# S4D convolution and gated GLU on one core: regrouped spectra transfers and a back transform in two rounded parts

## The chip, the cores and the metric

The kernel runs on one core of a Trainium2 chip. The metric is device time in microseconds (us) of one execution. A core has TensorE (PE, matrix products into the accumulator banks of PSUM), VectorE (DVE), ScalarE (ACT), GpSimd (POOL) and SyncE (SP, which here only issues transfers), and 16 DMA engines that move data between the on-chip memory (SBUF, 128 partitions) and DRAM. SP, ACT and POOL each have a queue of instructions of their own and can issue transfers from it.

## The reference, cut to what matters

```python
xn = layernorm(A_u)                                  # (1, 2048, 448)
dt = exp(log_dt); A = -exp(log_A_real) + 1j*A_imag   # A, C: (448, 256)
C  = (C_real + 1j*C_imag) * dt[:, None]
P  = exp((A*dt[:, None])[:, :, None] * arange(2048)) # (448, 256, 2048)
K  = 2 * einsum("dn,dnl->dl", C, P).real             # kernel of the convolution
y  = irfft(rfft(xn^T, 4096) * rfft(K, 4096), 4096)[:, :, :2048]^T + xn*D_skip
B  = (sigmoid(xn @ w_gate) * (xn @ w_up)) @ w_down   # 448 -> 1792 -> 448
return A_u + y + B                                   # all float32
```

## The kernel before, in words

Two generators are interleaved by weights that they yield: `conv` (the S4D part) and `glu` (the gated GLU). Their instructions go to the same engines. Within an engine's queue the order is fixed when the program is built; `issue_after` ties the matmuls of one generator behind those of the other.

**GLU.** It runs in two halves of the tokens. `gate` (line 661) makes the gate and up products: 11 matmuls of 512 columns for each of the two, since operands are split into a rounded part and a remainder (`wh`, `wl`, `xh`, `xl`, type F32R, which TensorE takes in one pass). ACT and DVE make `th`, `hf`, `hh`, `hl`. The down products `po` (line 781) are of 448 columns in the same split, and DVE adds them to `acc` (line 786).

**Convolution, first part** (`kgen`, to about 580 us). The kernel K is generated and put through the first stage of its transform, in 14 banks of 32 channels. After each bank `first_stage` writes the tile `sk` to the DRAM tensor `sk_d` (line 540, ACT queue, 512 KB each).

**Convolution, second part** (`spectra`, line 803). 16 steps: two halves h of the channels (224 each), and in each eight values of k (0, 4, ..., 28), four frequencies k1 to a step. One step is:

- `loads` (line 822), issued three steps ahead on SP: `sx`, the spectrum of the input, in two transfers (lines 826, 827); `tb`, a table (829); `skl`, the spectrum of the kernel (831). In `sk_d` a partition's part of `skl` lies in seven runs of 512 bytes.
- `there` (line 840): matmuls `sp` (line 854) into PSUM for two values of j, ACT copies one of them to `kc` (862), DVE multiplies the two complex spectra into `yy` (lines 865 to 868). The results of the two j lie in two tiles.
- `back` (line 872) for the step before: matmuls `pv` of `yy` with the table `bk` (line 880), both plain float32, 224 columns. Each of the 8 calls appears in the trace as two instructions. Partitions 0 to 63 and 64 to 127 are two independent products. ACT copies the results to `vt` (886), and four SP transfers write `vt` to `v_d` in DRAM (892).
- `turned` (line 894): one SP transfer of 448 KB brings the step's share of `v_d` back as `vp`, 16 partitions of 28,672 bytes, one step later. Its DRAM side is `v_d[h, k//4::8]`, 16 rows of 28,672 bytes each.

When all eight `vp` of a half are there, `last` (line 900) makes the final matmuls (909), DVE adds them to `ac` or `acc` (917), and `out` (line 214) writes finished tokens, taking SP, ACT and POOL in turn. For h = 0 the four calls of `last` come in the two steps after the last `turned` of that half is issued (`due = [n + 1]`, line 954). For h = 1 they come at the very end (line 799), behind the last GLU matmuls. GLU matmuls stand between `there` of a step and `back` of the next.

Of the kernel before, what the change touches and what calls it, by code (L numbers as in the profile page):

```python
# [20 lines left out]
D = 448  # L21
N = 256
F = 1792
NA = 32
NB = 64
NK1 = 32
# [13 lines left out]
H = D // 2  # L40
RB = 2
# [14 lines left out]
def _tables():  # L56

    a = np.arange(NA)[:, None]
    b = np.arange(NB)[:, None]
    k1 = np.arange(NK1)[None, :]  # L60
    ang = 2 * np.pi * ((a * (4 * k1 + 1)) % 128) / 128.0

    wk = np.zeros((4, NA, 2, 2, NK1))
    wx = np.zeros((4, NA, 2, NK1))
    for j in range(4):
        wk[j, :, 0, j % 2] = wx[j, :, 0] = np.cos(ang)
        wk[j, :, 1, j % 2] = wx[j, :, 1] = -np.sin(ang)
# [10 lines left out]
    split = lambda t: t.reshape(64, 2, 32).transpose(0, 2, 1)  # L78
    both = lambda r, i: np.stack([split(r), split(i)], 3).reshape(64, 128)
# [21 lines left out]
    f = lambda v, s: np.ascontiguousarray(v.reshape(s).astype(np.float32))  # L101
    return {
        "c_wk": f(wk, (128, 2, 64)),
        "c_wx": f(wx, (128, 64)),
        "c_tab": f(tab, (8, 128, 4, 128)),
        "c_bk": f(bk, (128, 2, 128)),
        "c_wf": f(wf, (128, 32, NA)),
        "c_sel": f(sel, (128, 2, 512)),
        "c_id": np.eye(128, dtype=np.float32),
    }  # L110
# [3 lines left out]
def s4d_glu_kernel(ctx, tc, io):  # L114
    nc = tc.nc
    hp = tc.high_priority
    v = nc.vector
# [93 lines left out]
    def blocks(t, g, b0, nb):  # L211
        return t[g, :, b0 // 8, b0 // 4 % 2, b0 % 4 : b0 % 4 + nb]

    def out(src, b0, h):

        ds = slice(H * h, H * h + H)
        for g in range(4):
            eng = (nc.sync, nc.scalar, nc.gpsimd)[outs[0] % 3]
# [206 lines left out]
    def kgen(pk):  # L425
# [95 lines left out]
        def first_stage(bank):  # L521

            ks, sk = tl["ks"], tl["sk"].rearrange("p k (s r j) -> p r k s j", r=2, j=2)

            pss = [
                psc[-1].tile([128, 8, 2, 32], F32, name="kp", bufs=1),
                psg.tile([128, 8, 2, 32], F32, name="kq", tag="gu", bufs=4),
            ]
            for s_ in range(8):
                for cc in range(2):  # L530
                    for r in range(2):
                        rows = slice(64 * r, 64 * r + 64)
# [7 lines left out]
            nc.scalar.dma_start(sk_d[:, bank], tl["sk"])  # L540

        with hp(HP):
            phase_load(0)
# [259 lines left out]
    def spectra(pf):  # L803
# [1 line left out]


        wf = const.tile([128, 32, NA], F32, name="wf", tag="sel", bufs=1)
        bk = const.tile([128, 2, 128], F32, name="bk", tag="wk", bufs=1)

        vp = {0: pf.tile([128, 32, H], F32, name="vp", bufs=1)}  # L810
        spare = {
            "vt": [pf.tile([128, 2, 2, H], F32, name="vt", bufs=2)],
            "pd": [pf.tile([128, 2, H], F32, name="pd", bufs=2)],
            "yy": [pf.tile([128, 2, H], F32, name="yy", bufs=4)],
            "kc": [pf.tile([128, 2, H], F32, name="kc", bufs=3)],
        }

        def work(n, sh, bufs):
            return spare[n].pop() if spare[n] else pf.tile(sh, F32, name=n, bufs=bufs)


        def loads(h, k):
            sx = pf.tile([128, 4, H], F32, name="sx", bufs=NLD)
            sk = pf.tile([128, 7, 4, 32], F32, name="skl", bufs=NLD)
            ds, gs = slice(H * h, H * h + H), slice(7 * h, 7 * h + 7)
# [5 lines left out]
            nc.sync.dma_start(sk, sk_d[:, gs, k : k + 4])  # L831
            return tb, sk, sx

        def bank(name):
            return psc[-1].tile([128, 2, H], F32, name=name, tag="sp", bufs=4)

        def after():
            return tc.issue_after(sp_mm[0].ins)

        def there(tb, sk, sx):  # L840

            ys_ = []
            for j in range(2):
                pss = []
                for src in (sk, sx):
# [14 lines left out]
                    if src is sk:  # L860
                        kc = work("kc", [128, 2, H], 3)
                        nc.scalar.copy(kc, ps)
                yy, pd = work("yy", [128, 2, H], 4), work("pd", [128, 2, H], 2)
                xt = pss[1]
                v.tensor_tensor(yy, kc, xt, ALU.mult)
                v.tensor_tensor(pd, kc, xt[:, ::-1], ALU.mult)
                v.tensor_tensor(yy[:, 0], yy[:, 0], yy[:, 1], ALU.subtract)
                v.tensor_tensor(yy[:, 1], pd[:, 0], pd[:, 1], ALU.add)
                ys_.append(yy)
            return ys_  # L870

        def back(h, k, ys_):
            vt = work("vt", [128, 2, 2, H], 2)
            pvs = [bank("pv") for _ in range(2)]
            with after():
                for j in range(2):
                    for e in range(2):
                        for i in range(2):
                            s = slice(64 * i, 64 * i + 64)
                            mm = nc.tensor.matmul(  # L880
                                pvs[i][:, j], bk[s, e], ys_[j][s, e], start=(e == 0), stop=(e == 1),
                                skip_group_check=True,
                            )
            sp_mm[:] = [mm]
            for i in range(2):
                nc.scalar.copy(vt[:, i], pvs[i])

            for j in range(2):
                for i in range(2):
                    k1 = k + 2 * j + i  # L890
                    to = v_d[h, 8 * (k1 % 4) + k1 // 4 :: 32]
                    nc.sync.dma_start(to.rearrange("r w d -> w r d"), vt[:, i, j])

        def turned(h, k):
            if h not in vp:
                vp[h] = pf.tile([128, 32, H], F32, name="vp", bufs=1)
            s = slice(k // 4, 128, 8)
            nc.sync.dma_start(vp[h][s], v_d[h, s])

        def last(h, m):  # L900

# [29 lines left out]
        for n, (h, k) in enumerate(steps):  # L931
# [167 lines left out]
```

## Time and profile before

| | |
|---|---|
| median of 3 runs | 773.14 us (771.35 to 775.21) |
| the profiled execution | 770.64 us |
| its span, first to last instruction | 768.9 us |
| mean granted TensorE clock | 0.968 |
| busy: PE, PEld, DVE, ACT, POOL | 705.4, 555.6, 557.4, 420.3, 359.7 us |
| bytes moved by DMA | 114.31 MB in 89575 packets |

The page of the profile gives each engine's busy time over the span, a strip of 40 equal slices, the DMA queues, the chain of work that ended last, and the costliest groups of instructions (line, engine, operation, output <- inputs, count | busy us, mean ns | idle time ahead of them and its releaser). PEld is the loading of weights into TensorE. A view by windows gives busy times in stretches of the span, the granted clock, the DMA share (mean busy share of the 16 DMA engines; packets of one engine may overlap, so it can pass 1) and GB/s. An "SPq" or "ACTq" row is an instruction of that queue, such as the issue of a transfer; where the chain says "DMA", the time runs from issue to landing.

### The profile page before, as it was taken

The page shows a single profiled execution, that of the slowest core. Times are in us where ns is not written, and L with a number is a line of the kernel's source. Part 1 is how long each engine was busy: PE and PEld are TensorE (multiplying, and loading weights), DVE is VectorE, ACT ScalarE, POOL GpSimd, SP SyncE. Part 2 cuts the span into 40 slices and gives each one's busy share as a digit, 9 for nine tenths or more (in the row PEclk, how much of TensorE's full clock was granted, in tenths as well). Part 3 has the DMA queues.
Part 4 walks back from the last instruction along what each step waited for, and adds up shares of the span by engine and source line. Part 5 has one row for each costly group of instructions (what it writes and reads, how often), then busy time and mean ns, then how long its engine had stood idle before and what let it go on. Part 6 is the DMA issues. An engine that isn't in the chain of part 4 may idle for free.

```text
span 768.9 us, 19294 instructions
## 1 busy us (share of the span) xinstructions
PE 705.4 (92%) x7868; PEld 555.6 (72%) x7868; DVE 557.4 (72%) x768; ACT 420.3 (55%) x647; POOL 359.7 (47%) x423
## 2 busy tenths in 40 slices
PE   2798899997999999898999999999899999969994
PEld 1575688876877877565788887887777778746783
DVE  5779996798978998778478977877864554634553
ACT  3636364767677976777387667686552322312320
POOL 1101036896785788853437584486555002331001
PEclk9998899999999999899999999999999999989998
DMA  9936337334323542363962232222157999999846
GB/s 205 227 81 187 95 93 230 101 122 151 120 70 126 185 135 67 108 189 92 269 182 69 68 124 66 90 94 67 41 142 199 283 240 238 230 241 242 189 127 161
DMA packets 89575, 114.31 MB, mean 149 GB/s; under 512 B 10896, under 2 KB 77456, under 8 KB 89232
## 3 DMA queue, kind: packets, MB, share of 16 engines
q1 hardware_dynamic: 80176, 92.36, 45.3%
q10 hardware_dynamic: 6736, 14.57, 6.3%
q0 software_dynamic: 2576, 6.17, 3.1%
q8 instruction: 62, 1.02, 0.6%
q14 instruction: 25, 0.20, 0.1%
HBM read 69.21 MB, written 43.84 MB: 147 GB/s over the span
## 4 chain that ended last, share of the span: by engine, by line
PE 40%; DMA 16%; DVE 15%; ACT 10%; POOL 9%; issue 7%; SPq 2%; ACTq 1%; POOLq 0%; DVEq 0%
PE gu L674 13%; PE po L781 11%; PE tr L506 4%; PE sp L854 4%; PE ko L582 3%; POOL me L483 3%; PE pv L880 2%; DVE pm L420 2%; DMA sx<-x_d 2%; DVE Et L569 2%; DVE Et L568 2%; ACT S L518 2%; POOL mf L483 2%; DVE Ft L570 2%; ACT S L516 1%
## 5 line engine op out<-in xcount | busy, mean ns | idle before, releaser
L483 POOL TENSOR_TENSOR me<-me,pm 128x32 f32<-128x32 f32 (+1 forms) x168 | 135.5, 807 | 99.5 <-DVE Et L569 88.1
L483 POOL TENSOR_TENSOR mf<-mf,pm 128x64 f32<-128x64 f32 (+1 forms) x112 | 118.0, 1054 | 4.5
L674 PE MATMUL gu<-xh,wh 128*128 128x512 f32 x336 | 101.3, 408 | 5.2 <-ACT xh L201 5.2
L569 DVE TENSOR_TENSOR Et<-me,S 128x1024 f32<-128x1024 f32 x56 | 80.0, 1429 | 24.5 <-ACT me L496 20.0
L674 PE MATMUL gu<-xh,wl 128*128 128x512 f32 x336 | 96.9, 394 | 0.0
L674 PE MATMUL gu<-xl,wh 128*128 128x512 f32 x336 | 96.6, 391 | 0.0
L781 PE MATMUL po<-dh,hh 128*128 128x448 f32 x224 | 87.3, 390 | 4.4 <-DVE acc L786 2.5
L568 DVE TENSOR_TENSOR Et<-me,S 128x1024 f32<-128x1024 f32 x56 | 77.9, 1391 | 16.8 <-ACT S L518 16.6
L690 ACT CAST hh<-hf 128x512 fp32r<-128x512 f32 x56 | 34.9, 623 | 98.9 <-DVE hf L685 74.7
L570 DVE TENSOR_TENSOR Ft<-mf,S 128x1024 f32<-128x1024 f32 x56 | 80.2, 1433 | 9.6 <-ACT S L518 7.4
L781 PE MATMUL po<-dl,hh 128*128 128x448 f32 x224 | 84.7, 379 | 0.0
L781 PE MATMUL po<-dh,hl 128*128 128x448 f32 x224 | 83.7, 376 | 0.0
L515 ACT ACTIVATE S<-tr 128x1024 f32<-128x1024 f32 x56 | 57.6, 1028 | 40.4 <-PE tr L506 34.9
L674 PEld LDWEIGHTS gu<-xh,wh 128*128 128x128 f32 x336 | 62.4, 193 | 22.1 <-ACT xh L201 6.7
L582 PEld LDWEIGHTS ko<-Et,Ft 128*32 128x32 f32 x3584 | 54.8, 112 | 28.4 <-issue 13.7
L674 PEld LDWEIGHTS gu<-xh,wl 128*128 128x128 f32 x336 | 63.2, 189 | 15.2 <-DVE pl L289 0.7
L674 PEld LDWEIGHTS gu<-xl,wh 128*128 128x128 f32 x336 | 63.2, 188 | 14.1 <-issue 0.7
L582 PE MATMUL ko<-Et,Ft 128*32 128x64 f32 x3584 | 64.9, 224 | 9.1 <-DVE Et L568 7.3
L685 DVE SCALAR_TENSOR_TENSOR hf<-th,gu 128x512 f32<-128x512 f32 x56 | 38.1, 681 | 42.3 <-PE gu L674 31.5
L506 PE MATMUL tr<-sel,ph 128*128 128x512 f32 x224 | 66.8, 419 | 1.7 <-ACT S L517 1.1
L786 DVE SCALAR_TENSOR_TENSOR acc<-po,acc 128x448 f32<-128x448 f32 x80 | 48.2, 617 | 24.4 <-PE po L781 24.3
L518 ACT ACTIVATE S<-S,hpi 128x1024 f32<-128x1024 f32 x56 | 65.5, 1169 | 0.0
(190 smaller groups left out, 1299.8 us busy)
## 6 DMA issues: line engine op xcount, KB each, us to landing
sk_d<-sk ACTq DMA_DIRECT2D x14, 512.0 KB
sx<-x_d SPq DMA_DIRECT2D x32, 224.0 KB
skl<-sk_d SPq DMA_DIRECT2D x16, 448.0 KB
v_d<-vt SPq DMA_DIRECT2D x64, 112.0 KB
vp<-v_d SPq DMA_DIRECT2D x16, 448.0 KB
wt_d<-wh SPq DMA_DIRECT2D x9, 512.0 KB
wt_d<-wl SPq DMA_DIRECT2D x9, 512.0 KB
wh<-wt_d SPq DMA_DIRECT2D x9, 512.0 KB
```

The costliest lines, as they stand in the source:

```text
L483: ins = nc.gpsimd.tensor_tensor(m[:, :, w + a : 2 * w : n], m[:, :, a:w:n], par(base + i).unsqueeze(2).to_broadcast([128, 4 * DC, w // n]) ...
L506: nc.tensor.matmul(ps[:, h], ph[:, cn % 2, 128 * h : 128 * h + 128], sel[:, i], start=(i == 0), stop=(i == 1),)
L515: nc.scalar.activation(rows(cs), pv, AF.Abs)
L518: sins[:] = [nc.scalar.activation(cs, cs, AF.Sin, scale=-TWO_PI, bias=hpi)]
L568: v.tensor_tensor(Et[:, :, :, 32:64], two(me[:, :, 32:64]), S[:, 1::-1], ALU.mult)
L569: v.tensor_tensor(Et[:, :, :, 0:32], two(me[:, :, 0:32]), S[:, 1:3, :, ::-1], ALU.mult)
L570: fts[:] = [v.tensor_tensor(Ft, two(mf), S[:, 3:5], ALU.mult)]
L582: mm = nc.tensor.matmul(ko[32 * j : 32 * j + 32, sl], Ft[:, cc, DC * h + 4 * q + j], Et[:, cc, DC * h + 4 * q + j], start=(k == 0), stop=( ...
L674: glu_mm[:] = [nc.tensor.matmul(ps, a_, b_, start=(n == 0), stop=(n == len(mm) - 1))]
L685: marks[1] = v.scalar_tensor_tensor(hf, th, 1.0, pgu[1], ALU.add, ALU.mult)
L781: glu_mm[:] = [nc.tensor.matmul(po, a_[:, bs], w_, start=(n == 0), stop=(n == 3 * fc - 1))]
L786: v.scalar_tensor_tensor(acc[:, b], po, 0.5, acc[:, b], ALU.mult, ALU.add)
```

## The change

Five things, all in or around `spectra`:

1. `sk_d`, `v_d` and the column orders of two tables (`c_wx`, `c_bk`) are laid out anew. `skl` becomes one run of 3,584 bytes per partition, while each bank's write of `sk` splits into eight runs of 512 bytes per partition. `sx` comes in one transfer instead of two. `vt` goes out in one transfer, issued from ACT, instead of four from SP. The load of `vp` stays one SP transfer into the same 16 partitions; its DRAM side is now a pattern of 4 (r) by 4 (q) runs of 28,672 bytes.
2. `back` takes the products as a rounded part `yh` and a remainder `yl`, and the table as `bk` and `bl`, all F32R: three terms (bk·yh, bl·yh, bk·yl), two tables e each, two halves of partitions, 448 columns per matmul (both j together). 12 matmuls in place of 8 calls that were 16 instructions.
3. ACT makes `yh` (a copy with rounding) and DVE makes `yl` (a subtraction), once for each j. `yh` and `yl` have one buffer each and `yy` two instead of four. `bl` is one more table to load.
4. The `out` transfers of half 0's finished `ac` go to SP alone.
5. `last` of half 0 starts one step later.

```diff
-    wx = np.zeros((4, NA, 2, NK1))
+    wx = np.zeros((4, NA, NK1, 2))
...
-    sk_d = dram.tile([128, D // 32, 32, 32], F32, name="sk_d")
+    sk_d = dram.tile([128, 2, 8, D // 64, 4, 32], F32, name="sk_d")
...
-    v_d = dram.tile([2, 128, 32, H], F32, name="v_d")
+    v_d = dram.tile([2, 8, 4, 4, 32, H], F32, name="v_d")
...
-            nc.scalar.dma_start(sk_d[:, bank], tl["sk"])
+            to = sk_d[:, bank // 7, :, bank % 7].rearrange("p e k d -> p e (k d)")
+            nc.scalar.dma_start(to, tl["sk"].rearrange("p (e k) d -> p e (k d)", k=4))
...
-            nc.sync.dma_start(sx[0:64], x1_d[k : k + 4, :, ds].rearrange("k b d -> b k d"))
-            nc.sync.dma_start(sx[64:128], x1_d[32 + k : 36 + k, :, ds].rearrange("k b d -> b k d"))
+            rows = x1_d.rearrange("(k c) b d -> (c b) k d", c=2)
+            nc.sync.dma_start(sx, rows[:, k : k + 4, ds])
...
-            nc.sync.dma_start(sk, sk_d[:, gs, k : k + 4])
+            nc.sync.dma_start(sk, sk_d[:, h, k // 4])
...
-                ys_.append(yy)
-            return ys_
+                nc.scalar.copy(yh[:, :, j], yy)
+                v.tensor_tensor(yl[:, :, j], yy, yh[:, :, j], ALU.subtract)
+            return yh, yl
...
+            terms = [(w, y, e) for w, y in ((bk, yh), (bl, yh), (bk, yl)) for e in range(2)]
             with after():
-                for j in range(2):
-                    for e in range(2):
-                        for i in range(2):
-                            s = slice(64 * i, 64 * i + 64)
-                            mm = nc.tensor.matmul(
-                                pvs[i][:, j], bk[s, e], ys_[j][s, e], start=(e == 0), stop=(e == 1),
-                                skip_group_check=True,
-                            )
+                for n, (w, y, e) in enumerate(terms):
+                    for i in range(2):
+                        s = slice(64 * i, 64 * i + 64)
+                        mm = nc.tensor.matmul(
+                            pvs[i], w[s, e], y[s, e], start=(n == 0), stop=(n + 1 == len(terms)),
+                            skip_group_check=True,
+                        )
             sp_mm[:] = [mm]
             for i in range(2):
-                nc.scalar.copy(vt[:, i], pvs[i])
-
-            for j in range(2):
-                for i in range(2):
-                    k1 = k + 2 * j + i
-                    to = v_d[h, 8 * (k1 % 4) + k1 // 4 :: 32]
-                    nc.sync.dma_start(to.rearrange("r w d -> w r d"), vt[:, i, j])
+                nc.scalar.copy(vt[:, :, i], pvs[i])
+            to = v_d[h, k // 4].rearrange("q r w d -> (r w) q d")
+            nc.scalar.dma_start(to, vt.rearrange("p j i d -> p (j i) d"))
...
-            s = slice(k // 4, 128, 8)
-            nc.sync.dma_start(vp[h][s], v_d[h, s])
+            src = v_d[h, k // 4].rearrange("q r w d -> r q (w d)")
+            nc.sync.dma_start(vp[h][k // 4 :: 8].rearrange("p w d -> p (w d)"), src)
...
-                    out(ac[:, 4 * q : 4 * q + 4], 4 * q, h)
+                    out(ac[:, 4 * q : 4 * q + 4], 4 * q, h, *([] if h else [[nc.sync]]))
...
+        nc.gpsimd.dma_start(bl, io["c_bl"])
...
-                    due = [n + 1]
+                    due = [n + 2]
```

More of the change, by code (lines that the diff above doesn't have):

```diff
@@ L63, in _tables @@
     wk = np.zeros((4, NA, 2, 2, NK1))
-    wx = np.zeros((4, NA, 2, NK1))
+    wx = np.zeros((4, NA, NK1, 2))
     for j in range(4):
-        wk[j, :, 0, j % 2] = wx[j, :, 0] = np.cos(ang)
-        wk[j, :, 1, j % 2] = wx[j, :, 1] = -np.sin(ang)
+        wk[j, :, 0, j % 2] = wx[j, :, :, 0] = np.cos(ang)
+        wk[j, :, 1, j % 2] = wx[j, :, :, 1] = -np.sin(ang)
     k2 = np.arange(64)[None, :]
@@ L77, in _tables @@
     al = 2 * np.pi * ((b * k2) % 64) / 64.0
-    split = lambda t: t.reshape(64, 2, 32).transpose(0, 2, 1)
-    both = lambda r, i: np.stack([split(r), split(i)], 3).reshape(64, 128)
+    both = lambda r, i: np.stack([r.reshape(64, 2, 32), i.reshape(64, 2, 32)], 2).reshape(64, 128)
     bk = np.zeros((2, 64, 2, 128))
@@ L101, in _tables @@
     f = lambda v, s: np.ascontiguousarray(v.reshape(s).astype(np.float32))
+    bits = bk.astype(np.float32).view(np.uint32)
+    bits = ((bits + 0x7FF + (bits >> 12 & 1)) & np.uint32(0xFFFFF000)).view(np.float32)
     return {
@@ L105, in _tables @@
         "c_tab": f(tab, (8, 128, 4, 128)),
-        "c_bk": f(bk, (128, 2, 128)),
+        "c_bk": f(bits, (128, 2, 128)),
+        "c_bl": f(bk - bits, (128, 2, 128)),
         "c_wf": f(wf, (128, 32, NA)),
@@ L212, in blocks, with out @@
         return t[g, :, b0 // 8, b0 // 4 % 2, b0 % 4 : b0 % 4 + nb]
-    def out(src, b0, h):
+    def out(src, b0, h, engs=(nc.sync, nc.scalar, nc.gpsimd)):
         ds = slice(H * h, H * h + H)
         for g in range(4):
-            eng = (nc.sync, nc.scalar, nc.gpsimd)[outs[0] % 3]
+            eng = engs[outs[0] % len(engs)]
             outs[0] += 1
@@ L807, in spectra @@
         wf = const.tile([128, 32, NA], F32, name="wf", tag="sel", bufs=1)
-        bk = const.tile([128, 2, 128], F32, name="bk", tag="wk", bufs=1)
+        bk = const.tile([128, 2, 128], F32R, name="bk", tag="wk", bufs=1)
+        bl = pg.tile([128, 2, 128], F32R, name="bl", tag="rd", bufs=RB)
         vp = {0: pf.tile([128, 32, H], F32, name="vp", bufs=1)}
@@ L813, in spectra, with work @@
             "pd": [pf.tile([128, 2, H], F32, name="pd", bufs=2)],
-            "yy": [pf.tile([128, 2, H], F32, name="yy", bufs=4)],
+            "yy": [pf.tile([128, 2, H], F32, name="yy", bufs=2)],
+            "yh": [pf.tile([128, 2, 2, H], F32R, name="yh", bufs=1)],
+            "yl": [pf.tile([128, 2, 2, H], F32R, name="yl", bufs=1)],
             "kc": [pf.tile([128, 2, H], F32, name="kc", bufs=3)],
         }
-        def work(n, sh, bufs):
-            return spare[n].pop() if spare[n] else pf.tile(sh, F32, name=n, bufs=bufs)
+        def work(n, sh, bufs, dt=F32):
+            return spare[n].pop() if spare[n] else pf.tile(sh, dt, name=n, bufs=bufs)
         def loads(h, k):
@@ L840, in there @@
         def there(tb, sk, sx):
-            ys_ = []
+            yh, yl = (work(n, [128, 2, 2, H], 1, F32R) for n in ("yh", "yl"))
             for j in range(2):
@@ L862, in there @@
                         nc.scalar.copy(kc, ps)
-                yy, pd = work("yy", [128, 2, H], 4), work("pd", [128, 2, H], 2)
+                yy, pd = work("yy", [128, 2, H], 2), work("pd", [128, 2, H], 2)
                 xt = pss[1]
```

3 lines of the change are left out of this document (2 added, 1 removed).

## The prediction, made before the changed kernel was run

> **What bounds the kernel now.** I read the page first: its list of transfers and its packet counts show what the change regroups.
>
> ```profile
> DMA packets 89575, 114.31 MB, mean 149 GB/s; under 512 B 10896, under 2 KB 77456, under 8 KB 89232
> ...
> sk_d<-sk ACTq DMA_DIRECT2D x14, 512.0 KB
> sx<-x_d SPq DMA_DIRECT2D x32, 224.0 KB
> skl<-sk_d SPq DMA_DIRECT2D x16, 448.0 KB
> v_d<-vt SPq DMA_DIRECT2D x64, 112.0 KB
> vp<-v_d SPq DMA_DIRECT2D x16, 448.0 KB
> ```
>
> 89575 - 89232 = 343 packets are of 8 KB or more, and 16 loads of vp in 16 rows of 28 KB make 256 of them: a vp load moves as 16 uncut packets. Next the view by windows, for the stretch in which the spectra run, and one ahead of it for comparison (columns: window, length, busy time and count of each engine, granted clock, DMA share, GB/s).
>
> ```profile
> 400.00:500.00 100.00, 99.53 (x1437) 82.68 (x1426) 84.07 (x93) 69.11 (x99) 61.76 (x76) 1.00 0.28 91
> 587.00:640.00 53.00, 51.62 (x381) 40.01 (x379) 29.17 (x61) 14.11 (x27) 4.24 (x4) 1.00 1.09 254
> 640.00:705.00 65.00, 56.13 (x504) 41.66 (x505) 30.70 (x62) 16.07 (x31) 21.82 (x26) 0.95 1.01 234
> 705.00:745.00 40.00, 40.00 (x291) 30.77 (x290) 21.53 (x44) 11.14 (x22) 0.00 (x0) 1.00 0.75 178
> 745.00:769.00 24.00, 13.56 (x173) 11.21 (x173) 7.46 (x13) 0.95 (x2) 4.37 (x8) 0.84 0.58 154
> ```
>
> Two things are full at once from 587 to 705 us: TensorE (51.62 of 53 us, 56.13 of 65) and the DMA engines (share 1.09 and 1.01). Earlier the DMA engines are mostly free (0.28). The chain of waits, in order of time, says which one the end hangs on.
>
> ```profile
> 641.47 8.39 DMA sx<-x_d
> ...
> 649.92 9.22 DMA skl<-sk_d
> ...
> 659.16 6.77 DMA v_d<-vt
> ...
> 666.00 8.57 DMA vp<-v_d
> ...
> 754.27 0.86 issue
> 755.13 1.09 PE pv L909 x32
> ```
>
> From 641 us on it is transfers, each needing the one before, 7 to 9 us from issue to landing; TensorE carries it again later, and the end is the last matmuls with additions and writes, 768.9 - 755.1 = 13.8 us. TensorE's own row for the one long stall, and a short step for what follows:
>
> ```profile
> 649.29 1.78 PE L880 MATMUL pv<-yy,bk 64*128 64x224 f32 x16
> 651.00 0.98 PE L854 MATMUL sp<-skl,tb 128*64 128x224 f32 x8
> ...
> 654.18 0.97 PE L674 MATMUL gu<-xh,wh 128*128 128x512 f32 x3
> ...
> 656.90 1.78 PE L880 MATMUL pv<-yy,bk 64*128 64x224 f32 x16
> ...
> 686.84 3.26 PE L909 MATMUL pv<-vp,wf 64*32 64x224 f32 x64 [7.25 <-DMA vp<-v_d]
> ```
>
> So the stage is one where TensorE just keeps up with full DMA engines, and loses 7.25 us where it must have a vp. What the change does to the DMA engines decides.
>
> **The change part by part.** *The price of a byte.* Over 587 to 745 us an engine was busy 53 x 1.09 + 65 x 1.01 + 40 x 0.75 = 153.4 us and moved (53 x 254 + 65 x 234 + 40 x 178) / 16 = 2,237 KB: 14.6 KB per busy us. In 400 to 500 us it was 91 / 0.28 / 16 = 20.3. These are my two ends.
>
> *The load of vp.* It keeps 448 KB (458,752 bytes) and 16 packets of 28.7 KB. Before, the DRAM side was 16 rows and the SBUF side 16 partitions, one packet for each DMA engine: 28.7 / 14.6 = 1.97 us. Now the DRAM side is 4 rows of 4. If a transfer is dealt to the engines by its outermost dimension, four engines carry four packets each: 4 x 1.97 = 7.87 us on those four, nothing on the other twelve. No row of this trace shows engine by engine where a transfer ran, so the ends are 1.97 us (spread as before), 4 x 28.7 / 20.3 = 5.65 us and 7.87 us. I take 7.87, since 14.6 is the rate of the very windows in which vp moves.
>
> The Trainium skill, page "DMA: Bandwidth & Descriptors", section "Why a DMA increments its semaphore by 16 and not by 1", states that rule: the number of engines is the largest one up to 16 that divides the slowest dimension of both sides, as the instruction carries it, and they are the lowest-numbered ones. By it 4 and 16 give four engines, always the same four, and the sum is the one below; without it the sum is that of the first rival. No run here shows it yet.
>
> ```profile
> L898 SPq DMA_DIRECT2D vp<-v_d x16: 511/518/1398, 609.5 to 750.2; - x16
> L540 ACTq DMA_DIRECT2D sk_d<-sk x14: 326/327/375, 191.5 to 583.0; - x14
> ```
>
> *skl and sk.* skl's seven runs of 512 bytes become one. Ends: no gain, or the step from 14.6 to 20.3 KB per us, 28.7 / 14.6 - 28.7 / 20.3 = 0.56 us per engine and load, 9.0 us for 16. I take 9.0, the upper end, since no other row has a price for a longer run; it is a tenth of what vp adds. The 14 writes of sk (191 to 583 us) lose at most as much per byte, 32.8 x (1/14.6 - 1/20.3) = 0.63 us each; a DMA share like 0.28 covers that, and nothing reads sk_d before the spectra begin.
>
> *Fewer issues.* One sx instead of two and one v_d write on ACT instead of four on SP free SP, which spends 2.60 us on the four:
>
> ```profile
> 645.89 0.51 SPq L898 DMA_DIRECT2D vp<-v_d  x1
> 646.44 2.60 SPq L892 DMA_DIRECT2D v_d<-vt  x4
> ...
> 649.92 0.38 SPq L831 DMA_DIRECT2D skl<-sk_d  x1
> ```
>
> ACT, busy 14.11 of 53 us, gains one issue per step, behind its own vt copies, so it waits for nothing else. The bytes of sx and v_d and their 896-byte runs stay. On the path I give these nothing: SP is the issuer, the engines are the limit. Were SP the limit, 2.6 us a step would be the gain.
>
> *back.* Instructions by form:
>
> ```profile
> L880 PE MATMUL pv<-yy,bk 64*128 64x224 f32 x256 | 28.5, 362 | 1.4 <-DMA bk<-in_c_bk_dram 1.4
> L865 DVE TENSOR_TENSOR yy<-kc,sp 128x448 f32<-128x448 f32 x32 | 19.8, 617 | 37.7 <-PE sp L854 36.6 <-ACT kc L862 1.1
> L862 ACT COPY kc<-sp 128x448 f32<-128x448 f32 x32 | 17.0, 533 | 14.9 <-PE sp L854 14.8
> ...
> 656.14 0.39 DVE L868 TENSOR_TENSOR yy<-pd 128x224 f32<-128x224 f32 x1
> ...
> 744.96 9.31 PE po L781 x45
> ```
>
> In the short step 16 instructions take 651.00 - 649.29 = 1.71 us, eight pairs (upper and lower 64 rows side by side) of 0.214 us. The new 448 columns in one pass are the form of po, 9.31 / 45 = 0.207 us each. Six pairs at 0.214 are 1.28 us: 0.43 us saved a step, 6.9 in 16. If the pairs did not run side by side, 12 x 0.207 = 2.48 us, 0.77 lost a step, 12.4 in all. I take the saving, since L880's own halves do run side by side.
>
> *yh and yl.* Two copies on ACT (0.53 us each by kc) and two subtractions on DVE (0.62 by yy) a step. The engines have room, but back now starts only when both j are rounded, as its first matmul spans both. In the short step DVE ends at 656.14 + 0.39 = 656.53, back starts at 656.90. Adding the first yl (0.62) and the second yh (0.53) gives 657.68, 0.8 us late, and the second yl and the handovers push it to perhaps 1.6. A step with two such groups of GLU matmuls between, 2 x 2.72 us, hides it. If about half of the 16 steps are as short as this one, it is 8 x 0.9 = 7 us; the ends are 0 and 8 x 1.6 = 13. It matters only where TensorE is the bound; where loads are late they cover it.
>
> *out and due.* This wait goes, with its 18.7 us of ACT standing still:
>
> ```profile
> ACT hh L690 <- DMA out_dram<-ac: 18.7, 1, 18.7
> ```
>
> and last of half 0 comes a step later, so the 7.25 us stall can shrink to nothing if vp is on time. The price is that SP holds back its later loads while it waits for DVE's ac; with loads three steps ahead I cost it at nothing, and at up to the 7.25 if that lead is used up. bl, 128 KB on POOL, rides beside bk.
>
> **The sum.** Four engines need, until the point that was 745 us: 153.4 - 9.0 + 15 x (7.87 - 1.97) = 232.9 busy us (15 of the 16 vp are issued by then, the last at 750.2). The share in the two full windows was (57.8 + 65.7) / 118 = 1.05, so 232.9 / 1.05 = 222 us: 587 + 222 = 809. That takes all other traffic at its old price. At the other end, with twelve engines idle half the time, everything but vp goes at 20.3 and the share is 1.09: (232.9 - 118.1) x 14.6 / 20.3 = 82.6, plus 118.1, over 1.09 = 184: 771. I take the middle, 790. Then come the last vp, 7.87 / 1.05 = 7.5, and the tail of 13.8, which the vp now releases: 811. The time outside the span is 770.64 - 768.9 = 1.7: 813 beside the profiled 770.64. The median of the runs is 2.5 above that execution, so **815 us**, with 796 and 834 from the two ends. TensorE's saving in back doesn't show in it; it waits longer for loads.
>
> **The rivals.**
>
> *First: vp still spreads over 16 engines, or its place costs nothing; faster.* Then TensorE is the bound: 7.25 and 6.9 us go, 7 come back as waits for yh and yl: 773.1 - 7 = 766, down to 759 without the waits. For it: the loads run three steps ahead, and a vp is needed only in last. Against: all these loads share SP's queue and the DMA engines were full (1.09) with vp spread, so there is no room. It decides as long as a vp load takes less than about 4 us on its busiest engine: 15 x 2 = 30 busy us more is what the 0.75 window, the 9.0 of skl and the three steps' lead can take up.
>
> *Second: four engines, but each at 20.3 KB per us.* (153.4 - 29.6 - 9.0) x 14.6 / 20.3 + 15 x 5.65 = 167.4, over 1.09 = 154: the engines are done at 741, about with TensorE. With a last vp 3.7 us longer and some waits, 768 to 785, say 776. For it: the other traffic leaves room on the shared memory. Against: the row of the last vp. It is issued at 750.2 and the matmuls that need it start at 755.13 with no wait for it left, in a window with share 0.58; even that quiet load doesn't prove a faster packet.
>
> *Third: the halves of back do not run side by side.* 12.4 + 7 - 7.25 gives 785 if vp spreads. Against: L880.
>
> **How the numbers follow.** Four engines at about the old rate 0.70 (796 to 834, some 0.05 of it above), spread vp 0.15, four fast engines 0.11, serial halves 0.04. The range 774 to 834 leaves out most of the first rival and the top, 0.2. What a measurement can tell from no change is about 0.5%, 769.3 to 777.0: faster 0.19 (first rival and a part of the second), same 0.05, slower 0.76.
>
> **What would show it.** Right: the window after 600 us has a DMA share well under 1 (twelve engines waiting) while TensorE is idle for several us in most steps, released by sx, skl or tb; a step like the short one above lasts 11 us or more instead of 7.6; the last matmuls wait for vp. back shows 12 instructions in 1.28 us, and ACT's 18.7 us wait is gone. Wrong: TensorE stays busy through 705 us and the last vp lands under 5 us after its issue; then four engines were not used, or were not short of time. If TensorE's idle time stands ahead of back with yh or yl as releaser, the operand chain was the cost.

## The result, and the profile after it

The changed kernel takes 806.35 us (median of 4 runs, 803.68 to 810.02) beside 773.79 us for the kernel before: ratio 1.043, 95% interval [1.038, 1.048]. It is slower by 33 us. The profiled execution took 803.68 us, its span is 801.9 us, the mean granted clock 0.951 (before: 0.968).

First the view by windows of the changed kernel, with the columns as in the prediction.

```profile
400.00:500.00 100.00, 98.65 (x1385) 81.67 (x1384) 83.00 (x90) 72.67 (x104) 64.37 (x77) 1.00 0.31 96
587.00:640.00 53.00, 48.31 (x349) 36.01 (x348) 29.61 (x60) 19.18 (x36) 8.43 (x10) 1.00 0.81 221
640.00:705.00 65.00, 42.12 (x266) 31.07 (x266) 32.31 (x58) 17.28 (x33) 19.07 (x22) 0.82 0.82 187
705.00:745.00 40.00, 39.72 (x364) 28.26 (x365) 25.30 (x51) 14.59 (x27) 1.73 (x2) 0.95 0.70 209
745.00:802.00 57.00, 35.89 (x319) 27.79 (x317) 22.08 (x44) 9.54 (x18) 4.42 (x8) 0.87 0.40 124
```

Between 400 and 500 us little has changed (TensorE 98.65 us of 100 beside 99.53). In 640 to 705 us TensorE is busy for 42.12 us where it was 56.13, and the DMA share has fallen from 1.01 to 0.82. Neither is full now: both wait. The clock that TensorE is granted falls as well (0.95 to 0.82), and what comes after a long gap is slower: the 12 instructions of a `back` take 2.61 us there and mostly 1.5 us elsewhere. TensorE's list of waits names the gaps, and ACT's names what is behind them.

```profile
PE pv L889 <- ACT yh L876: 27.2, 8, 8.5
...
PE pv L914 <- DMA out_dram<-acc: 9.9, 1, 9.9
```

```profile
ACT kc L869 <- DMA vp<-v_d: 12.7, 3, 6.2
...
ACT kc L869 <- DMA skl<-sk_d: 8.4, 1, 8.4
```

None of these rows stood in the lists of before. TensorE waits 27.2 us for `yh`, and ACT, which makes it, stands in front of `kc`, allegedly for a `vp`. That is odd: a copy from PSUM to `kc` doesn't read `vp`. ACT's timeline of the changed kernel, and TensorE's beside it, show what stands there.

```profile
663.72 0.97 ACT L895 COPY vt<-pv 128x448 f32<-128x448 f32 x2 [1.08 <-PE pv L889]
670.52 0.37 ACTq L897 DMA_DIRECT2D v_d<-vt  x1
670.93 0.97 ACT L869 COPY kc<-sp 128x448 f32<-128x448 f32 x2 [6.25 <-DMA vp<-v_d]
674.13 0.56 ACT L876 CAST yh<-yy 128x448 fp32r<-128x448 f32 x1 [2.23 <-DVE yy L875]
677.42 0.56 ACT L876 CAST yh<-yy 128x448 fp32r<-128x448 f32 x1 [2.73 <-DVE yy L875]
```

```profile
651.04 1.11 PE L889 MATMUL pv<-yh,bk 64*128 64x448 f32 x4 [6.29 <-ACT yh L876]
...
678.03 1.11 PE L889 MATMUL pv<-yh,bk 64*128 64x448 f32 x4 [8.46 <-ACT yh L876]
```

`vt` is ready at 663.72 + 0.97 = 664.7, but its issue to `v_d` goes out only at 670.52. ACT works in order, so `kc` and `yh` stand behind that issue, and TensorE behind `yh`. The chain of waits shows it twice: at 644.93 the issue goes as `skl` lands, at 670.52 as a `vp` lands. Between them stands the next `vp`, which reads what `v_d` wrote. Each wait is longer than before (6.77 us for `v_d` and 8.57 for `vp` there).

```profile
630.92 13.93 DMA skl<-sk_d
644.93 12.09 DMA v_d<-vt
657.04 13.41 DMA vp<-v_d
670.52 12.87 DMA v_d<-vt
683.41 13.77 DMA vp<-v_d
...
726.73 1.42 PE pv L889 x12
...
768.19 9.33 PE po L785 x45
...
778.58 8.19 DMA out_dram<-acc
...
787.42 3.34 PE pv L914 x64
```

The `vp` issued at 657.04 lands at 670.45, and 0.07 us later ACT's issue goes. Why the one waits for the other can be read in the trace's records of the transfers, which give the semaphore each transfer counts its landing on:

```
waiting issue        semaphore   transfer before it on the same semaphore   landed
644.93 ACT v_d<-vt   110         630.92 SP skl<-sk_d                        644.85
643.96 SP  tb        101         630.30 SP vp<-v_d                          643.9
655.12 ACT v_d<-vt   115         633.15 SP vp<-v_d                          655.0
670.52 ACT v_d<-vt   112         657.04 SP vp<-v_d                          670.45
697.26 ACT v_d<-vt   114         683.41 SP vp<-v_d                          697.2
```

The program gives SP's and ACT's transfers eight semaphores in turn (POOL has eight others), and an issue stands until the transfer before it on its semaphore has landed. It is a property of how this program is built. Before, ACT issued no loads or writes of the spectra, and a `vp` had landed in 5 to 11 us; now it takes 9 to 23, and the eighth issue after it comes sooner than that. So the changed kernel goes in rounds: `vp` holds the issue of `v_d`, and the next `vp` needs what that `v_d` writes. ACT's issues at 644.93, 670.52 and 697.26 are 25.6 and 26.7 us apart and there is one more between each two, so a round is two steps.

A ledger from the starts of the first, fifth, tenth and last `back`, of the last matmuls and from the span, read off TensorE's timeline, puts the 33.0 us where they are. Before, those starts are 594.09, 629.29, 674.62, 743.17 and 755.13; after, they are 597.96, 634.41, 704.77, 766.45 and 787.42. Up to the first `back` it is 3.9 us more, and 1.3 more to the fifth. From the fifth to the tenth 70.4 us in place of 45.3: **25.0 more**. From there to the last `back` 6.9 us less, about the stall of 7.25 us on `vp`, which is gone. From the last `back` to the last matmuls **9.0 more**, then 0.7. The 9.0 belong to the wait of 9.9 us that the list puts down to `out_dram<-acc`. The last `vp` is issued at 774.47, by the records of the transfers it lands at 787.1, and the matmuls that read it start at 787.42, so it is the one they wait for.

### The profile page after: what moved, and what is told of

The parts are those of the page before. It is cut to its first block, busy times and chain, and to the rows that moved or that the text cites. A ratio compares the mean times of both kernels' runs of the same rounds, so it can differ in the third digit from the quotient of the medians.

```text
span 801.9 us, 19106 instructions
## 1 busy us (share of the span) xinstructions
PE 706.0 (88%) x7804; PEld 551.7 (69%) x7804; DVE 576.8 (72%) x800; ACT 438.3 (55%) x679; POOL 361.9 (45%) x422
## 3 DMA queue, kind: packets, MB, share of 16 engines
q8 instruction: 62, 1.02, 0.6%
## 4 chain that ended last, share of the span: by engine, by line
PE 41%; DMA 18%; DVE 15%; POOL 10%; ACT 7%; issue 6%; SPq 1%; ACTq 1%; POOLq 0%; DVEq 0%
PE gu L678 16%; PE po L785 9%; PE tr L509 4%; PE ko L586 4%; POOL me L486 4%; DMA vp<-v_d 3%; DMA v_d<-vt 3%; PE sp L861 3%; POOL mf L486 2%; PE pv L889 2%; DVE pm L423 2%; DMA skl<-sk_d 2%; DVE Et L572 1%; ACT S L521 1%; DVE Et L573 1%
## 5 line engine op out<-in xcount | busy, mean ns | idle before, releaser
L586 PEld LDWEIGHTS ko<-Et,Ft 128*32 128x32 f32 x3584 | 54.4, 111 | 30.1 <-issue 13.8
L586 PE MATMUL ko<-Et,Ft 128*32 128x64 f32 x3584 | 64.5, 223 | 10.8 <-DVE Et L572 8.0
L872 DVE TENSOR_TENSOR yy<-kc,sp 128x448 f32<-128x448 f32 x32 | 19.8, 617 | 62.1 <-ACT kc L869 53.8
```

The costliest lines, as they stand in the source:

```text
L586: mm = nc.tensor.matmul(ko[32 * j : 32 * j + 32, sl], Ft[:, cc, DC * h + 4 * q + j], Et[:, cc, DC * h + 4 * q + j], start=(k == 0), stop=( ...
```

## The experiments

Before any of them I held three theories. **T1**: four engines for `vp` cost the time. **T2**: the issue of `v_d` from ACT costs it. **T3**: the longer chain of operands, yy, `yh`, `yl`, costs it. A fourth question was what the regrouped loads bring. (The first expectations call them 1, 2 and 3.) Each run's ratio is to the kernel before on the same chip.

**1. The DRAM side of vp alone, in the kernel before** (label b_vp4).

```diff
-    v_d = dram.tile([2, 128, 32, H], F32, name="v_d")
+    v_d = dram.tile([2, 8, 4, 4, 32, H], F32, name="v_d")
...
-                    to = v_d[h, 8 * (k1 % 4) + k1 // 4 :: 32]
+                    to = v_d[h, k1 // 4, k1 % 4]
...
-            nc.sync.dma_start(vp[h][s], v_d[h, s])
+            src = v_d[h, k // 4].rearrange("q r w d -> r q (w d)")
+            nc.sync.dma_start(vp[h][k // 4 :: 8].rearrange("p w d -> p (w d)"), src)
```

> The kernel before with one edit: v_d laid out by k/4, q, r, w, so that the load of vp has a DRAM side of 4 by 4 runs; its four writes on SP, the plain float32 back and all else stay. Theory 1 (four DMA engines carry all of vp and run out of time): 800 to 820 us, a vp landing 9 us or more after its issue in four steps, the DMA share in 640 to 705 us well under 1, TensorE waiting for loads. Theory 2 (the v_d write on ACT's queue is what stalls the changed kernel) and theory 3 (the rounded parts yh and yl make back wait) have nothing to act on here: 772 to 776 us.

Measured: 826.9 us, ratio 1.075 [1.069, 1.080], 6.9 us above theory 1's range. That one pattern costs more than the whole change. In its lists of waits (TensorE's, then ACT's) there is no `yh`, which this kernel doesn't have:

```profile
PE sp L854 <- ACT vt L886: 22.8, 8, 5.0
PE pv L909 <- DMA out_dram<-acc: 22.7, 1, 22.7
PE pv L909 <- DMA vp<-v_d: 7.8, 1, 7.8
```

```profile
ACT vt L886 <- DMA v_d<-vt: 58.6, 9, 11.2
```

Here ACT cannot write the next `vt`, since the `v_d` write out of that buffer hasn't landed: SP issued it right behind a `vp` load, and it lands with that load (issued at 666.97 and 667.56, landed at 679.4 and 679.6). T1 holds, though the loss is larger than I had put it.

**2. The changed kernel, its one v_d write from SP** (a_vd_on_sp): `nc.scalar.dma_start(to, ...)` becomes `nc.sync.dma_start(to, ...)`.

> The changed kernel with its one v_d write a step issued from SP instead of ACT; vp keeps its 4 by 4 runs. Theory 1: four engines still carry vp, 798 to 815 us. Theory 2: ACT no longer stands still before kc, 765 to 785 us. Theory 3: no change, 803 to 810 us.

Measured: 830.95 us, ratio 1.077 [1.071, 1.082], outside what any theory gave. T2 as I had put it falls: with a slow `vp`, taking the write off ACT makes things worse by 25 us. SP's issues of the last `vp` loads show the pace, and TensorE's last matmuls what waits for it:

```profile
771.87 0.52 SPq L903 DMA_DIRECT2D vp<-v_d  x1
782.56 0.52 SPq L903 DMA_DIRECT2D vp<-v_d  x1
793.93 0.52 SPq L903 DMA_DIRECT2D vp<-v_d  x1
805.09 0.53 SPq L903 DMA_DIRECT2D vp<-v_d  x1
```

```profile
814.41 5.99 PE L914 MATMUL pv<-vp,wf 64*32 64x224 f32 x128 [23.73 <-DMA out_dram<-acc]
```

A step takes 10.7 to 11.4 us there, with little else moving. The chain of this run shows why:

```profile
772.48 10.06 DMA v_d<-vt
...
783.17 10.74 DMA v_d<-vt
793.93 0.52 SPq L903
...
794.54 10.54 DMA v_d<-vt
```

A `v_d` write is issued right behind a `vp` load on the same queue and lands 1.2 to 2.0 us after it (at 782.5, 793.9 and 805.1, where by the landing records the loads land at 781.4, 791.9 and 803.9). The next `vp` load, which reads what that write wrote, is issued 0.02 us after its landing. The landing records also show why the write is late. It posts 16 landings: of the write issued at 772.48 twelve come 2.6 to 2.7 us after the issue, and four 8.8 to 10.1 us after it, about 1 us behind the four landings of the `vp` load ahead of it. So a quarter of the write comes behind the load, and the rest does not. The two make a round of 11 us to a step. TensorE's steps in the kernel before took (743.17 - 594.09) / 15 = 9.9 us on average. Where the round is the longer one it sets the pace, and not the sum of the bytes.

**3 and 4. vp spread over 16 rows, v_d from ACT or from SP** (a_vp16_act, a_vp16_sp). The DRAM order becomes k // 4, r, q, w; the write of `vt` then takes four transfers of 32 partitions.

```diff
-            to = v_d[h, k // 4].rearrange("q r w d -> (r w) q d")
-            nc.scalar.dma_start(to, vt.rearrange("p j i d -> p (j i) d"))
+            for r in range(4):
+                to = v_d[h, k // 4, r].rearrange("q w d -> w q d")
+                nc.scalar.dma_start(to, vt[32 * r : 32 * r + 32].rearrange("p j i d -> p (j i) d"))
...
-            src = v_d[h, k // 4].rearrange("q r w d -> r q (w d)")
+            src = v_d[h, k // 4].rearrange("r q w d -> (r q) (w d)")
```

(In a_vp16_sp it is `nc.sync` in the third added line.)

> The changed kernel with v_d laid out by k/4, r, q, w: the load of vp has a DRAM side of 16 rows again, and vt goes out in four transfers of 32 partitions, still from ACT. Theory 1: the loss goes and the gains show, 755 to 768 us. Theory 2: ACT still issues the writes, four instead of one, and waits with them; some of the loss stays, 775 to 800 us. Theory 3: 795 to 806 us.

> The same as the run before, with the four v_d writes issued from SP as in the kernel before. Theory 1: 755 to 768 us, within 3 us of the run with the writes on ACT. Theory 2: 755 to 768 us, and 10 us or more below the run with the writes on ACT. Theory 3: 795 to 806 us.

Measured: 792.9 us, 1.030 [1.025, 1.036], from ACT; 773.57 us, 1.001 [0.998, 1.005], from SP. With the spread load the order turns round: SP is better than ACT by 19 us. So there are two costs and they work on each other. The 792.9 us lie in theory 2's range; the 773.57 us lie in no theory's range, though 19 us below the run on ACT, as theory 2 had it. In a_vp16_act TensorE waits 21.0 us for `yh`. ACT's list puts 10.8 us ahead of `kc`, in four waits, down to landings of `v_d`, but beside its issues these gaps are something else:

```profile
633.36 2.49 ACTq L898 DMA_DIRECT2D v_d<-vt  x4
635.89 0.97 ACT L869 COPY kc<-sp 128x448 f32<-128x448 f32 x2 [2.56 <-DMA v_d<-vt]
```

The gap is the time of the four issues themselves, here 2.49 us (1.78 to 3.95 us in the 16 steps, 0.37 us for the one issue of the changed kernel). So with the spread load ACT pays for four issues, and with the 4 by 4 load it waits for landings. But the spread kernel doesn't gain: the 766 us of the prediction's first rival isn't reached.

**5. vp on eight engines** (a_vp8_sp). As a_vp16_sp, with a DRAM side of 8 by 2 (the rows of the table `wf` are put into the matching order).

```diff
-    v_d = dram.tile([2, 8, 4, 4, 32, H], F32, name="v_d")
+    v_d = dram.tile([2, 8, 2, 2, 4, 32, H], F32, name="v_d")
...
-                to = v_d[h, k // 4, r].rearrange("q w d -> w q d")
+                to = v_d[h, k // 4, r % 2, r // 2].rearrange("q w d -> w q d")
...
-            src = v_d[h, k // 4].rearrange("r q w d -> (r q) (w d)")
+            src = v_d[h, k // 4].rearrange("o t q w d -> (t q) o (w d)")
```

> The 773.6 us run (spread vp, v_d from SP) with the vp load's DRAM side laid out as 8 runs of 2 rows and not as 16 rows (the rows of vp and of its table wf in the matching order). With 4 engines the same issue took 831 us. Theory A (a threshold, as the prediction's first rival puts it, about 4 us per vp load): 8 engines carry 2 packets each, about 3.9 us, just below it: 772 to 782 us. Theory B (each packet in series adds, without a threshold): a third of the way from 16 to 4 engines, 787 to 800 us. If the load does not go to 8 engines, its landings say so: 8 of them a load, where 16 rows post 16 and 4 x 4 post 4.

Measured: 772.5 us, 1.000 [0.996, 1.004]: theory A, a threshold. The landing records give the load's price without other traffic, from issue to last landing, in the last steps of each run: 4.3 to 4.6 us for 16 rows, 6.7 to 6.8 for 8 by 2, 9.0 to 10.0 for 4 by 4. SP's issues of the 8 by 2 load are spaced by the step, not by the load:

```profile
736.09 0.58 SPq L904 DMA_DIRECT2D vp<-v_d  x1
744.07 0.59 SPq L904 DMA_DIRECT2D vp<-v_d  x1
752.39 0.58 SPq L904 DMA_DIRECT2D vp<-v_d  x1
```

8.0 and 8.3 us are below TensorE's 9.9; the 4 by 4's 11 are above. It isn't quite free: in this profiled execution the last matmuls wait 8.7 us, where a_vp16_sp shows 1.2.

**6 and 7. v_d from POOL**, which has semaphores of its own (a_vd_on_pool with the 4 by 4 load, a_vp16_pool with 16 rows): `nc.gpsimd.dma_start` in the place of `nc.scalar.dma_start`.

> The changed kernel with its one v_d write per step issued from POOL and not from ACT; the vp load stays on four DMA engines. Theory A: what PE lost in the changed kernel came through ACT, whose v_d issue stood until an earlier SP load had landed (kc and yh, and PE's 27.2 us for yh, behind it): off ACT, the 27 us of waits for yh fall to 5 to 9 us and the time to 780 to 792 us. Theory B: the four engines of the vp load are the bound whoever issues v_d: the waits turn up at sx, skl, tb or at the end, 800 to 832 us.

> The spread vp load (16 rows) with the four v_d writes from POOL. From ACT they took 792.9 us, from SP 773.6 us. Theory A (ACT held by its issue is what the 19 us between those two are): like SP, 770 to 778 us, with at most 9 us of waits for yh and hf. Theory B (the writes landing later or later vp loads, wherever SP does not issue them): 785 to 795 us. POOL's own casts of raw weights may stand behind its issue; if so they show as waits of gu for wl.

Measured: 793.05 us, 1.025 [1.019, 1.031], and 777.36 us, 1.006 [1.003, 1.009]. TensorE's waits with the 4 by 4 load:

```profile
PE pv L914 <- DMA out_dram<-acc: 13.8, 1, 13.8
PE pv L889 <- ACT yh L876: 7.6, 6, 3.7
PE sp L861 <- ACT vt L895: 6.6, 1, 6.6
```

The waits for `yh` fall from 27.2 to 7.6 us, as theory A said, and the time by 13 us. With 16 rows POOL is within 4 us of SP, and 15.5 under ACT. The 777.36 us are theory A's too. So the issue on ACT is a cost in itself: 13 us with the slow load, where it waits for landings, and 15 to 19 with the spread one, where there are four issues a step. But 793 is 1 us above theory A's range, and the load keeps its own price: against 16 rows the 4 by 4 load costs 13 us with `v_d` from ACT (806.35 less 792.9), 16 from POOL and 57 from SP, though with 16 rows `v_d` goes out in four transfers and not in one. Both theories are true, each for its part.

**8. The regrouped loads alone, in the kernel before** (b_regroup): the edits to `c_wx`, `sk_d`, `sx` and `skl` in the diff above, and nothing else of it.

> The kernel before with the regrouped sk and x1 transfers alone (one sx load instead of two, skl in one run per partition); back, vp and v_d as before. Theory A: TensorE's only long wait there was for vp, behind v_d, so shorter skl and sx loads can at most shorten that wait of 7.3 us: 767 to 774 us, the share of the DMA engines in 640 to 705 us falls from 1.01 to about 0.85. Theory B: the DMA engines were the bound with TensorE, so the whole 9 us count: 762 to 766 us.

Measured: 761.83 us, ratio 0.987 [0.983, 0.991]. It is faster than both kernels by more than its uncertainty. Its windows:

```profile
587.00:640.00 53.00, 51.93 (x380) 39.92 (x379) 31.82 (x60) 14.09 (x27) 5.84 (x7) 1.00 0.92 282
640.00:705.00 65.00, 64.15 (x568) 47.26 (x567) 39.23 (x71) 18.81 (x36) 21.85 (x26) 1.00 0.86 235
```

The DMA share falls from 1.09 and 1.01 to 0.92 and 0.86, TensorE goes from 56.13 to 64.15 us of 65, and the stall of 7.25 us on `vp` isn't in its list any more. The share is what theory A gave, the time theory B's to 0.2 us: 9.9 us are saved. But the engines were relieved of more than that, 53 x (1.09 - 0.92) + 65 x (1.01 - 0.86) = 18.8 busy us in these two windows. What there was to gain is TensorE's idle time: 1.38 + 8.87 us in them before, 1.07 + 0.85 us now, 8.3 us less. So the loads had held TensorE up, and now it is TensorE that is full. Whether it was the bytes on the engines isn't shown: the edit also takes away one of SP's nine issues a step, where eight semaphores go round, and no run parts the two.

**9. The rounded back alone, in the kernel before** (b_back): the edits to `back`, `bk`, `bl`, `yh`, `yl`, in the old column order.

> The kernel before with the rounded back alone (12 matmuls of 448 columns, yh and yl), all transfers as before. Theory A: saves 0.3 us x 16 = 5 us of TensorE and gives back 5 to 9 us in waits for yh: 770 to 780 us. Theory B (the chain is covered): 766 to 769 us.

Measured: 775.07 us, 1.002 [0.998, 1.005]: no change, as theory A gave. But the profile gives more than one reason. Its waits:

```profile
PE pv L889 <- ACT yh L876: 3.6, 4, 1.3
...
PE pv L918 <- DMA vp<-v_d: 2.5, 1, 2.5
PE sp L861 <- ACT vt L895: 2.3, 1, 2.3
```

Its DMA share in 640 to 705 us is 1.02, as full as before, and time saved on TensorE may have turned into waits for transfers; this run doesn't part the two.

**10. The spread kernel with the old float32 back** (s_back32): a_vp16_sp with the 16 matmuls of 224 columns, and no `yh`, `yl`, `bl`.

> The run with the spread vp load and the four writes from SP (773.6 us), with the float32 back transform of the kernel before put back: 16 matmuls of 224 columns, no yh, no yl. Theory A: the rounded back saves 0.3 us a step on TensorE and loses it in its longer chain (5.1 us of waits for yh and 3.6 us behind hf in the 773.6 us run, and the slower clock after them), so without it the time is lower though TensorE has 5 us more work: 763 to 769 us, no wait of a back matmul above 1 us in 640 to 705 us. Theory B: the transfers, not the chain, set those gaps: the gaps stay and the 5 us are added: 775 to 781 us.

Measured: 762.06 us, 0.988 [0.983, 0.993]. Theory A, and 0.9 us better than its range. So of the two halves of the change it was the rounded back that held a_vp16_sp at 773.6. And it is no faster than b_regroup (761.83), which has neither the later `last` nor `out` on SP: no run shows a gain of those two. In a_vp16_sp the gaps are ahead of `back`; its list, and then TensorE, DVE and POOL at one of them:

```profile
PE pv L889 <- ACT yh L876: 5.1, 3, 3.2
PE pv L889 <- DVE hf L689: 3.6, 1, 3.6
```

```profile
660.83 1.19 PE L889 MATMUL pv<-yh,bk 64*128 64x448 f32 x4 [3.58 <-DVE hf L689]
```

```profile
654.60 0.39 DVE L875 TENSOR_TENSOR yy<-pd 128x224 f32<-128x224 f32 x1
...
657.65 2.52 DVE L875 TENSOR_TENSOR yy<-pd 128x224 f32<-128x224 f32 x1
```

```profile
657.34 2.59 POOL L739 TENSOR_TENSOR wl<-wraw,wh 128x1024 fp32r<-128x1024 f32 x1
```

A DVE addition that took 0.39 us takes 2.52 while POOL subtracts for the weights of the GLU, and `yh`, `yl` and `hf` queue up behind it. With the float32 `back` POOL does the same work, but the chain ends two instructions earlier: in s_back32 the longest such wait is 1.0 us.

**11. The rounded back one step later** (s_late). Two `yh` and two `yl`; for their room `kc` also holds the products, with the two multiplications in turned order, and `kc` has two buffers and `pd` one.

```diff
-            if prev is not None:
-                back(*prev)
+            old = None
+            if len(held_) > 1:
+                old = held_.pop(0)
+                back(*old)
...
-            prev = (h, k, cur)
+            held_.append((h, k, cur))
...
-                yy, pd = work("yy", [128, 2, H], 2), work("pd", [128, 2, H], 2)
+                yy, pd = kc, work("pd", [128, 2, H], 1)
```

> The 773.6 us run with each back transform one step later, two yh and two yl (kc holds the products, pd once). Theory A: the chain yy, yh, yl then has a whole step of cover, the waits for yh and behind hf (8.7 us) and the slow clock after them go: 761 to 767 us. Theory B: the gaps come from transfers, or the later vt, vp and last matmuls lengthen the end by as much: 771 to 778 us.

Measured: 764.78 us, 0.992 [0.989, 0.995]: theory A. No wait for `yh` is left, and its window has no gap:

```profile
640.00:705.00 65.00, 64.30 (x489) 46.89 (x485) 49.02 (x84) 26.93 (x51) 21.31 (x24) 1.00 0.84 239
```

With that T3 is shown for the gaps of a_vp16_sp. Still this is no better than the float32 back (762.06), though TensorE has 12 instructions a step in place of 16. A wait of 2.5 us ahead of the last matmuls takes part of it:

```profile
748.09 4.30 PE L914 MATMUL pv<-vp,wf 64*32 64x224 f32 x128 [2.52 <-issue]
```

**12. The last step does two backs** (s_late2): s_late with this, so that less stands at the end.

```diff
+            if n + 1 == len(steps):
+                wait.append(old[:2])
+                old = held_.pop(0)
+                back(*old)
```

> The run with the back transform one step later (764.8 us), with the last step doing two back transforms, so that one back, one v_d write and one vp load fewer stand at the end. Theory A (its 2.5 us wait ahead of the last matmuls came from the four v_d writes and the vp load of two steps standing in SP's queue): 761 to 763.5 us. Theory B (that wait comes from the last load itself): 764 to 766 us.

Measured: 765.09 us, 0.990 [0.985, 0.994]. Theory B: the wait is still there (2.96 us). The views name no releaser for it, but by the landing records the last `vp` lands at 749.39 and the last matmuls start at 749.58 (in s_late 747.89 and 748.09). That a rounded `back` can beat the float32 one here isn't shown by any run.

## Why the prediction was right, and where it was not

The forecast was slower, 815 us in 774 to 834; it is 806. By its steps:

- **What bounds the kernel**: right in that the loads held TensorE up: b_regroup relieves the loads, and then TensorE is full. But the chain was misread. It is not "transfers, each needing the one before": `skl` doesn't read `sx`, and the write of `v_d` doesn't read `skl`. By the records of before, `sx` (641.47), `skl` (649.92) and `v_d` (659.16) count on one semaphore, 111, and `skl` and `v_d` are issued 0.06 and 0.02 us after the landing ahead of them. The wait that later held ACT stood in that chain already, in SP's queue.
- **vp on four engines**: right in its cause, which b_vp4 and a_vp8_sp show, and mis-sized. The 7.87 us per load came from 28.7 KB at 14.6 KB per us, 1.97 us a packet. The 256 packets of 28,672 bytes took 1.61 us on average in the changed kernel (2.05 before): 6.4 us a load. With that the four engines' sum is 153.4 - 9.0 + 15 x (6.4 - 1.97) = 210.9 busy us, 788 at one end, 751 at the other ((210.9 - 96) x 14.6 / 20.3 + 96 = 178.6, over 1.09 = 164), and the forecast 769 + 6.1 + 13.8 + 1.7 + 2.5 = 793.
- **The sum itself** went by the wrong quantity. It added up bytes on four engines; the runs show a round of `v_d` and `vp`, 11 us against TensorE's 9.9 a step, with 8 engines below it, and in the changed kernel a round of 26 us for two steps, through ACT's issue. That a_vd_on_sp and b_vp4 take 827 to 831 us while much the same bytes take 793 with `v_d` on POOL can't come out of a sum of busy time.
- **skl and sk in longer runs**: nearly right in size. By the packet records from 587 us on, a load of `skl` took an engine 56 packets of 37 ns, 2.05 us, before, and 8 of 192 ns, 1.54 us, in b_regroup: 0.5 us less, 8 us in 16 loads and not 9.0. What the prediction put at nothing is that the other packets got faster too (896 bytes: 58 ns before, 45 in b_regroup); why, no run shows.
- **Fewer issues**: here the prediction failed. It said that ACT's issue stands "behind its own vt copies, so it waits for nothing else". It stands for the landing of an SP load, 12.7 + 8.4 us in ACT's list, and costs 13 us (806.35 less 793.05). The mis-sized vp put 22 us too much into the total (815 less 793) and this unpriced wait left 13 out, so that 815 comes within 9 us of 806 is in part luck. That 793 turns up both as the corrected sum and as the POOL run is no proof of either.
- **back**: 12 instructions in 1.42 us, not 1.28, where the clock is full. A pair of 448 columns takes 0.237 us and not 0.214. So 0.29 us a step is saved, 4.6 in all and not 6.9. After a long gap they take 2.6 us.
- **yh and yl**: the 7 us were right in size where loads don't cover them: 5.1 + 3.6 us in a_vp16_sp, plus the slow clock behind each gap. Its reason was half right. It priced the added instructions, 0.8 to 1.6 us a short step, and the long gaps come where POOL's work stretches DVE's.
- **out and due**: right in that ACT's 18.7 us are gone and so are the 7.25. But in b_regroup, without these edits, the 7.25 are gone as well and ACT's wait there is 6.3 us, so the edits are not shown to be the reason.
- **What would show it**: the DMA share fell, the steps got long (14.1 us on average from the fifth to the tenth) and the last matmuls wait for `vp`. But the idle time's releaser was `yh`, which the prediction had listed as the sign that the operand chain was the cost. That sign misled: `yh` was late because ACT had been standing at an issue.
- **First rival**: as a mechanism it is right up to its threshold (8 engines cost nothing in time, at 2 packets of 1.89 us each), and its price was wrong: 773.6, not 766. Its 6.9 us of gain were 4.6, and the 7.25 saved on the stall came back as gaps with a slow clock.

## What to carry to other kernels

When a wait's named releaser has nothing to do with the waiting instruction, look at what stands ahead of it in the same queue: an issue that cannot go blocks the engine's own work as surely as a missing operand. Before changing the shape of a load, ask for the round trip of the step it belongs to and compare that with the step of the busiest engine: here the load was free below it, and above it every step paid. And try the parts of a change one at a time: here a part worth 10 us by itself was hidden behind one that by itself cost 55.

## What the runs showed of the hardware that was not expected

**The same engines each time.** In the changed kernel's records a load of `vp` posts four landings, in a_vp8_sp eight and in before sixteen (the first two also one record about 1 us after the issue). Four loads issued within 1.8 us of each other (from 734.13 us on) land 4.3 to 4.4 us apart; with 16 rows (a_vp16_sp) such a burst lands 1.1 to 2.2 us apart. Four loads on sixteen different engines would have landed together. The other transfers show it too: of the 16 landings of the `v_d` write issued at 670.52 twelve come within 3.2 us and four after 10.8 to 12.9 us; of `skl` issued at 630.92 twelve come within 5.2 us and four after 13.3 to 13.9. The Trainium skill, page "DMA: Bandwidth & Descriptors", section "Why a DMA increments its semaphore by 16 and not by 1", says that the number of engines is the largest one up to 16 that divides the slowest dimension of both sides, and that for transfers such as SP's they are the lowest-numbered. The records agree for 16, 8 and 4 landings, and the late fours speak for the same engines each time; which ones they are, no record here says.

**A faster packet, a slower load.** With four engines one packet of 28 KB takes 1.61 us on average, with sixteen 2.05, yet the load takes twice as long or more.

**DVE slowed by POOL.** DVE's 0.39 us addition of two SBUF tiles took 2.52 us while POOL subtracted two SBUF tiles for 2.59 us, and 2.47 beside 2.41 at the next such place. In the changed kernel a product with one operand in PSUM, issued at 674.02 during such a subtraction (673.93 to 676.30), kept its 0.61 us, and the 0.39 us one of two SBUF tiles behind it took 2.00. The Trainium skill, page "SBUF — State Buffer", section "Who interferes with whom", says that a DVE instruction with two SBUF inputs contends with a GpSimd one that reads SBUF, and calls the ports that they share an exclusive lock. The trace agrees at both places: DVE's addition ends 0.24 and 0.25 us after POOL's subtraction.
